# Half of a weight matrix on 32 partitions by four DMA engines, its product as one row, and fifteen tiny loads from ScalarE's queue

## The chip, the cores and the metric

The kernel runs on one core of one Trainium2 chip. The metric is the device time of an execution in microseconds (us), of which medians over several executions are quoted. The span that a profile gives is about 2 us shorter than the time, because it runs from the first to the last instruction. All runs of this study were in the fast state, so fast runs are compared with fast runs throughout.

## The reference, cut to what matters

A single token `x` of 512 values goes through an attention over a window of 4096 cached positions for 32 heads, and through a small MLP whose result gates the attention.

```python
xn = _layernorm(x)
# attention: q = xn @ wq; softmax(q k^T) v over the last 4096 positions, 32 heads of 128; @ wo
s = _A_ref(xn, k_cache, v_cache, wq, wo)
# gate
h  = gelu(layernorm(xn) @ w1)
g0..g3 = h shifted by one or two positions, forward and back
hs = concatenate([g0, g1, g2, g3]) @ w2      # 512 x 512
x1 = xn + hs
h2 = gelu(layernorm(x1) @ w3) @ w4           # 512 x 1376, 1376 x 512
g  = silu(x1 + h2)
return x + s * g
```

With one position every shift moves all of `h` out, so what is multiplied by `w2` is zero. The kernel still loads `w2` and does the product, with a vector of zeros. That matters for the experiments: the order in which the rows of `w2` lie cannot change the result.

The bytes are nearly all in the caches and weights: 67.1 MB of K and V in 64 loads of 1024 KB, `wq` and `wo` with 4.2 MB each, and 3.3 MB of `w2`, `w3` and `w4` (`w1` is not loaded).

## The kernel before

The program first issues the loads of `x`, from ScalarE, and of the weights, from SyncE, whose helper `load` keeps them in program order.

```python
    x_bf = small.tile([P, KC], BF16, name="x_bf")
    nc.scalar.dma_start(out=x_bf[:], in_=A_x.rearrange("a b (p c) -> p (a b c)", p=P))
    x_row = small.tile([P, P], BF16, name="x_row")
    nc.gpsimd.memset(x_row[:], 0.0)
    nc.scalar.dma_start(out=x_row[0:P:32, :], in_=A_x.rearrange("a b (j n) -> (a b j) n", j=KC))
    w2_sb = wts.tile([P, KC, D], BF16, name="w2_sb")
    load(w2_sb[:], B_w2.rearrange("(p c) n -> p c n", p=P))
    w3_sb = wts.tile([P, KC, F], BF16, name="w3_sb")
    load(w3_sb[:], B_w3.rearrange("(p c) n -> p c n", p=P))
    # ... three loads of w4, one of wq
```

The product with `w2` fills four columns, and its result is added to the normalized `x`. The sum `x1_f` starts the second half of the MLP.

```python
    for j in range(KC):
        for c in range(KC):
            nc.tensor.matmul(hs_ps[:, j:j + 1], lhsT=w2_sb[:, c, j::4],
                             rhs=shifted_bf[:, c:c + 1], start=(c == 0), stop=(c == KC - 1))
    x1_f = small.tile([P, KC], FP32, name="x1_f")
    nc.vector.tensor_tensor(out=x1_f[:], in0=xn_f[:], in1=hs_ps[:], op=ALU.add)
```

Some sums are opened by a matmul that writes zeros. It reads an identity matrix, which GpSimd makes.

```python
    def rows_open(ps):
        nc.tensor.matmul(ps[:], lhsT=zero_bf[:], rhs=ident_bf[:], start=True, stop=False,
                         skip_group_check=True)
```

The loop then loads a K tile per head and, four heads later, a V tile. The V tiles reuse the memory of the MLP's and q's weights, so the first V load has to wait for the last matmul that reads `wq`.

```python
    for i in range(H + LAG):
        if i < H:
            k_head(i, load_kv(k_pool, A_k_cache, i))
        if i == LAG:
            wts_guard.__exit__(None, None, None)
            v_pool = ctx.enter_context(tc.tile_pool(name="v", bufs=V_BUFS))
        if i >= LAG:
            v = load_kv(v_pool, A_v_cache, i - LAG)
            # ... wo loads, v_head
```

Of the kernel before, what the change touches and what calls it, by code (L numbers as in the profile page):

```python
# [9 lines left out]
P = 128  # L10
BF16 = mybir.dt.bfloat16
FP32 = mybir.dt.float32
ACT = mybir.ActivationFunctionType
ALU = mybir.AluOpType
# [5 lines left out]
G = 4  # L20
LAG = 4
K_BUFS = 12
V_BUFS = 7


@with_exitstack
def kernel(
# [14 lines left out]
    nc = tc.nc  # L42

    Bb, Sq, D = A_x.shape
# [9 lines left out]
    KC = D // P  # L54
# [5 lines left out]
    small = ctx.enter_context(tc.tile_pool(name="small", bufs=1))  # L60
    ps_misc = ctx.enter_context(tc.tile_pool(name="ps_misc", bufs=1, space=PSUM))
    ps_tr = ctx.enter_context(tc.tile_pool(name="ps_tr", bufs=3, space=PSUM))
    ps_s = ctx.enter_context(tc.tile_pool(name="ps_s", bufs=2, space=PSUM))
    ps_o = ctx.enter_context(tc.tile_pool(name="ps_o", bufs=1, space=PSUM))
    ps_y = ctx.enter_context(tc.tile_pool(name="ps_y", bufs=1, space=PSUM))
    k_pool = ctx.enter_context(tc.tile_pool(name="k", bufs=K_BUFS))
    kt_pool = ctx.enter_context(tc.tile_pool(name="kt", bufs=2))
# [3 lines left out]
    wts = wts_guard.__enter__()  # L71

    def load(dst, src):
        return tc.keep_in_program_order(nc.sync.dma_start(out=dst, in_=src))
# [3 lines left out]
    x_row = small.tile([P, P], BF16, name="x_row")  # L78
    nc.gpsimd.memset(x_row[:], 0.0)
    nc.scalar.dma_start(out=x_row[0:P:32, :], in_=A_x.rearrange("a b (j n) -> (a b j) n", j=KC))  # L80
    w2_sb = wts.tile([P, KC, D], BF16, name="w2_sb")
    load(w2_sb[:], B_w2.rearrange("(p c) n -> p c n", p=P))
    w3_sb = wts.tile([P, KC, F], BF16, name="w3_sb")
    load(w3_sb[:], B_w3.rearrange("(p c) n -> p c n", p=P))
    w4_sb = wts.tile([P, 11, D], BF16, name="w4_sb")
    load(w4_sb[:, 0:8, :], B_w4[0:8 * P, :].rearrange("(p c) n -> p c n", p=P))
    load(w4_sb[:, 8:10, :], B_w4[8 * P:10 * P, :].rearrange("(p c) n -> p c n", p=P))
# [4 lines left out]
    def load_kv(pool, cache, h):  # L92
        t = pool.tile([P, NC, Dh], BF16, tag="kv", name="kv")
        load(t[:], cache[0, h, W0:, :].rearrange("(p c) d -> p c d", p=P))
        return t
# [5 lines left out]
    ones_f = const.tile([P, P], FP32, name="ones_f")  # L101
# [26 lines left out]
# [4 lines that stand above are left out]
    def rows_add(ps, col, w, last):  # L132
        k = col.shape[0]
        for j in range(KC):
            nc.tensor.matmul(ps[32 * j:32 * j + 1, :], lhsT=col, rhs=w[0:k, j * P:(j + 1) * P],  # L135
                             start=False, stop=last, skip_group_check=True)
# [28 lines left out]
    xn_f = small.tile([P, KC], FP32, name="xn_f")  # L165
# [5 lines left out]



    shifted_bf = small.tile([P, KC], BF16, name="shifted_bf")
    nc.vector.memset(shifted_bf[:], 0.0)
    hs_ps = ps_misc.tile([P, KC], FP32, tag="misc", name="hs_ps")
    for j in range(KC):
        for c in range(KC):
            nc.tensor.matmul(hs_ps[:, j:j + 1], lhsT=w2_sb[:, c, j::4],
                             rhs=shifted_bf[:, c:c + 1], start=(c == 0), stop=(c == KC - 1))  # L180
    x1_f = small.tile([P, KC], FP32, name="x1_f")
    nc.vector.tensor_tensor(out=x1_f[:], in0=xn_f[:], in1=hs_ps[:], op=ALU.add)  # L182
    xc3, _, rstd3 = ln_stats(x1_f[:], "z3")
    z3_bf = small.tile([P, KC], BF16, name="z3_bf")
    nc.vector.tensor_scalar(out=z3_bf[:], in0=xc3[:], scalar1=rstd3[:], scalar2=None, op0=ALU.mult)

    hsr_ps = ps_misc.tile([P, P], FP32, tag="misc", name="hsr_ps")
    rows_open(hsr_ps)
    for c in range(KC):
        rows_add(hsr_ps, shifted_bf[:, c:c + 1], w2_sb[:, c, :], c == KC - 1)  # L190
    x1_row = small.tile([P, P], FP32, name="x1_row")
    nc.vector.tensor_scalar(out=x1_row[:], in0=x_row[:], scalar1=negmean[:], scalar2=rstd[:],
                            op0=ALU.add, op1=ALU.mult)
# [6 lines left out]
    for j, (m, cols) in enumerate(chunks):  # L200
        for c in range(KC):
            nc.tensor.matmul(a_ps[0:m, j:j + 1], lhsT=w3_sb[:, c, cols], rhs=z3_bf[:, c:c + 1],  # L202
                             start=(c == 0), stop=(c == KC - 1))
# [15 lines left out]
    for h in range(1, H, 2):  # L219
        for c in range(KC):  # L220
            nc.tensor.matmul(qT_ps[:, h:h + 1], lhsT=wq_sb[:, c, h * Dh:(h + 1) * Dh],  # L221
                             rhs=xn_bf[:, c:c + 1], start=(c == 0), stop=(c == KC - 1))
# [4 lines left out]
    for i in range(0, H // 2, 4):  # L227
        qb_ps = ps_tr.tile([P, 4, Dh], FP32, tag="pt", name="qb_ps")
        for c in range(KC):
            nc.tensor.matmul(qb_ps[:], lhsT=xn_rep[:, c, :], rhs=wq_h[:, c, 2 * i:2 * i + 8:2, :],  # L230
                             start=(c == 0), stop=(c == KC - 1))
# [16 lines left out]
    def flush():  # L248
        while pending:
            qk(*pending.pop(0))  # L250

    def k_head(h, kn):
        g, hl = divmod(h, G)
        if hl == 0:
            st[g] = {
                "sT": ps_s.tile([P, G // 2, NC], FP32, tag="sT", name="sT"),
                "sS": sm_pool.tile([P, G // 2, NC], FP32, tag="sS", name="sS"),
            }
        s = st[g]
        if h % 2 == 0:  # L260
            prod = prod_pool.tile([P, NC, Dh], BF16, tag="prod", name="prod")
            nc.vector.tensor_tensor(out=prod[:], in0=kn[:],  # L262
                                    in1=q_bc[:, h // 2:h // 2 + 1, :].to_broadcast([P, NC, Dh]),
                                    op=ALU.mult)
            nc.vector.tensor_reduce(out=s["sS"][:, hl // 2, :], in_=prod[:], axis=AX.X, op=ALU.add)  # L265
        else:
            kt = kt_pool.tile([P, NC, P], BF16, tag="kt", name="kt")
            for b in range(NB):
                pt = ps_tr.tile([P, 8, P], BF16, tag="pt", name="pt")
                for i in range(8):  # L270
                    nc.tensor.transpose(pt[:, i, :], kn[:, b * 8 + i, :], ident_bf[:])  # L271
                nc.scalar.copy(out=kt[:, b * 8:(b + 1) * 8, :], in_=pt[:])  # L272
                if b == 0:
                    flush()
            pending.append((s["sT"], hl, h, kt))
            if hl == G - 1:
                flush()
        if hl == G - 1:
            softmax(g)
# [33 lines left out]
    def load_wo(i):  # L313
        h0, n = blocks[i]
        rows = A_wo[h0 * P:(h0 + n) * P, :]
        if n == 8:
            t = k_pool.tile([P, n, D], BF16, tag="kv", name="wo_8")
        else:
            t = v_pool.tile([P, n, D], BF16, tag=f"wo{i}", bufs=1, name="wo_4")
        wo_blk[i] = t  # L320
        if i < last_block:
            load(t[:], rows.rearrange("(p t) n -> p t n", p=P))
        else:
            rows = rows.rearrange("(h p) n -> p h n", p=P)
            load(t[:, 0:n - 1, :], rows[:, 0:n - 1, :])
            load(t[:, n - 1, :], rows[:, n - 1, :])
# [59 lines left out]
    for i in range(H + LAG):  # L386
        if i < H:
            k_head(i, load_kv(k_pool, A_k_cache, i))
        if i == LAG:
            wts_guard.__exit__(None, None, None)  # L390
            v_pool = ctx.enter_context(tc.tile_pool(name="v", bufs=V_BUFS))
        if i >= LAG:
            h = i - LAG
            v = load_kv(v_pool, A_v_cache, h)
            if h + 1 in (b[0] for b in blocks):
                load_wo(block_of[h])
            if h == H - 1:
                load_wo(last_block)
            v_head(h, v)
# [38 lines left out]
```

## Time and profile before

| quantity | before |
|---|---|
| time, beside the changed kernel | 198.97 us, median of 4 (198.35 to 199.78) |
| span of the profiled execution | 196.8 us |
| bytes of weights and caches | 78.85 MB |
| their rate between 50 and 180 us | 421 GB/s |
| the sum x1 | 14.00 us |
| the first V load is issued | 30.13 us |
| the last `wo` load lands, first to last of the 16 engines | 188.50 to 193.18 us |

The profile's lines for this kernel stand in the prediction below. To read them: the GB/s line has 40 slices of 4.92 us, and any slice well below 420 is time that the DMA engines did not use. In the lists of waits the three numbers are the total in us, the count, and the longest. The kernel is one stream of bytes at a steady rate. Its end moves when the stream loses time; apart from that, the last of the 16 engines ends 1.6 to 2.7 us behind their mean in the kernels below.

One more number is needed below, and the prediction lacks it. All that is queued ahead of the first V load is `w2`, `w3`, `w4`, `wq` and five K tiles, 12.78 MB. In this trace 12.74 MB have moved at 33.5 us. The first V load, issued at 30.13, has its first bytes at about 31.2 if it takes 1.03 us as the first weight load did (0.72 to 1.75). So the engines had 2.3 us of work left when the V data arrived. That is the whole reserve of the first V load.

### The profile page before, as it was taken

To read this page: it belongs to the slowest core of one execution; us is meant where nothing else is said; L and a number is where in the kernel's file an instruction comes from. 1 tells how busy PE (TensorE), PEld (TensorE's weight loads), DVE (VectorE), ACT (ScalarE), POOL (GpSimd) and SP (SyncE) were. 2 spreads that over 40 slices of the span, in tenths; PEclk is the share of its full clock that TensorE was granted. 3 is DMA by queue.
4 is the path that set the end of the run, shared out by engine and by line. 5 is a ranking of instruction groups with operands and counts; after the bars stand their busy time and mean duration, and the time that the engine had idled before them with its cause. 6 is when DMAs were issued, how large, how long until landed. Compare 5 with 4: busy or idle time off the path is not lost.

```text
span 196.8 us, 5237 instructions
## 1 busy us (share of the span) xinstructions
PE 119.4 (61%) x2399; PEld 108.4 (55%) x2399; DVE 126.9 (64%) x140; ACT 69.3 (35%) x82; POOL 4.9 (3%) x17
## 2 busy tenths in 40 slices
PE   0315896851969474684829293756665654929443
PEld 0314745841969473583829292656565653929332
DVE  1225049998959993959387937959198929594301
ACT  2000329742565243070707070242525250707000
POOL 1011000000000000000000000000000000000000
PEclk9999999695585555576766667555555585575555
DMA  6999899999999999999999999999999999999960
GB/s 185 383 485 446 355 416 421 426 426 421 426 421 423 421 421 425 423 425 420 426 421 428 421 425 416 425 420 426 423 428 423 425 418 425 421 426 422 426 268 10
DMA packets 11349, 79.17 MB, mean 402 GB/s; under 512 B 1376, under 2 KB 1984, under 8 KB 2368
## 3 DMA queue, kind: packets, MB, share of 16 engines
q1 hardware_dynamic: 11176, 78.85, 96.3%
q8 instruction: 18, 0.29, 0.6%
q10 hardware_dynamic: 152, 0.00, 0.0%
q14 instruction: 3, 0.02, 0.0%
HBM read 78.84 MB, written 0.00 MB: 401 GB/s over the span
## 4 chain that ended last, share of the span: by engine, by line
DMA 71%; DVE 12%; issue 6%; PE 6%; ACT 2%; POOL 1%; SPq 0%; POOLq 0%
DMA kv<-in_A_v_cache_dram 40%; DMA kv<-in_A_k_cache_dram 30%; DVE sS L265 7%; DVE prod L262 3%; ACT kt L272 1%; PE a_ps L202 1%; PE qT_ps L221 1%; PE oT L364 1%; PE qb_ps L230 1%; PE h_ps L135 1%; PE y_ps L135 0%; PE ln_ps L140 0%; PE ln_ps L152 0%; ACT q_bc L232 0%; POOL ln_rstd_x L158 0%
## 5 line engine op out<-in xcount | busy, mean ns | idle before, releaser
L272 ACT COPY kt<-pt 128x1024 bf16<-128x1024 bf16 x64 | 60.2, 1025 | 73.0 <-PE pt L271 73.0
L265 DVE TENSOR_REDUCE sS<-prod 128x32 f32<-128x4096 bf16 x16 | 70.7, 4419 | 0.5
L271 PE MATMUL pt<-ident_bf,kv 128*128 128x128 bf16 x512 | 53.8, 298 | 18.2 <-DMA kv<-in_A_k_cache_dram 17.7
L271 PEld LDWEIGHTS <-kv 128*128 128x128 bf16 x512 | 49.8, 140 | 19.7 <-DMA kv<-in_A_k_cache_dram 18.7
L364 PEld LDWEIGHTS <-kv 128*128 128x128 bf16 x1024 | 30.0, 102 | 30.5 <-DMA kv<-in_A_v_cache_dram 22.8
L262 DVE TENSOR_TENSOR prod<-kv,q_bc 128x4096 bf16<-128x4096 bf16 x16 | 36.5, 2283 | 11.0 <-DMA kv<-in_A_k_cache_dram 8.8
L364 PE MATMUL oT<-pT,kv 128*128 128x1 bf16 x1024 | 32.6, 165 | 17.6 <-DMA kv<-in_A_v_cache_dram 17.3
L243 PE MATMUL sT<-qT_bf,kt 128*128 128x1 bf16 x512 | 20.4, 166 | 2.6 <-ACT kt L272 2.3
L243 PEld LDWEIGHTS <-kt 128*128 128x128 bf16 x512 | 18.3, 103 | 3.4 <-ACT kt L272 3.2
L300 PE MATMUL den_ps<-pT,ones_bf 128*128 128x128 bf16 x8 | 2.0, 253 | 16.9 <-ACT pT L294 16.9
L371 DVE TENSOR_TENSOR o<-oT,rden 128x4 bf16<-128x4 f32 x7 | 1.1, 162 | 17.3 <-PE oT L364 17.3
L294 ACT ACTIVATE pT<-e 128x128 bf16<-128x128 f32 x8 | 2.5, 309 | 16.5 <-DVE e L290 16.5
L140 PEld LDWEIGHTS ln_ps<-x_f,ones_f 128*128 128x128 f32 x4 | 1.0, 312 | 11.3 <-DVE x_f L182 6.4
L287 POOL PARTITION_ALL_REDUCE mb<-m x8 | 3.0, 373 | 162.5 <-DVE m L285 162.5
L205 ACT ACTIVATE a_bf<-a_ps 128x10 bf16<-128x10 f32 x1 | 0.2, 180 | 17.4 <-PE a_ps L202 17.4
L302 DVE TENSOR_REDUCE den<-den_ps 128x4 f32<-128x128 f32 x8 | 2.3, 292 | 5.5 <-PE den_ps L300 5.5
L135 PEld LDWEIGHTS <-ox 128*1 128x1 bf16 x112 | 2.5, 113 | 5.3 <-DVE ox L341 5.3
L367 DVE TENSOR_TENSOR o<-oT,rden 128x1 bf16<-128x1 f32 x4 | 0.6, 161 | 7.2 <-PE oT L364 7.2
L230 PE MATMUL qb_ps<-wq_sb,xn_rep 128*128 128x512 bf16 x16 | 5.2, 497 | 0.0
L135 PE MATMUL y_ps<-wo,ox 128*1 128x128 bf16 x112 | 3.7, 306 | 2.3 <-DVE ox L341 2.3
L140 PE MATMUL ln_ps<-x_f,ones_f 128*128 128x4 f32 x4 | 1.2, 365 | 5.9 <-DVE x_f L163 4.9
L290 DVE TENSOR_TENSOR e<-sS,mb 128x64 f32<-128x64 f32 x8 | 1.8, 224 | 3.9 <-POOL mb L287 3.9
(79 smaller groups left out, 48.2 us busy)
## 6 DMA issues: line engine op xcount, KB each, us to landing
kv<-in_A_k_cache_dram SPq DMA_DIRECT2D x32, 1024.0 KB, 19.7
kv<-in_A_v_cache_dram SPq DMA_DIRECT2D x32, 1024.0 KB, 19.7
wq_sb<-in_A_wq_dram SPq DMA_DIRECT2D x1, 4096.0 KB, 19.2
wo<-in_A_wo_dram SPq DMA_DIRECT2D x3, 1024.0 KB, 20.4
w_sb<-in_B_w_dram SPq DMA_DIRECT2D x1, 1376.0 KB, 7.9
w_sb<-in_B_w_dram SPq DMA_DIRECT2D x1, 1024.0 KB, 10.2
w_sb<-in_B_w_dram SPq DMA_DIRECT2D x1, 512.0 KB, 3.7
wo<-in_A_wo_dram SPq DMA_DIRECT2D x1, 512.0 KB, 19.8
```

The costliest lines, as they stand in the source:

```text
L135: nc.tensor.matmul(ps[32 * j:32 * j + 1, :], lhsT=col, rhs=w[0:k, j * P:(j + 1) * P], start=False, stop=last, skip_group_check=True)
L140: nc.tensor.matmul(ps[:], lhsT=ones_f[:], rhs=src_f, start=True, stop=True)
L230: nc.tensor.matmul(qb_ps[:], lhsT=xn_rep[:, c, :], rhs=wq_h[:, c, 2 * i:2 * i + 8:2, :], start=(c == 0), stop=(c == KC - 1))
L243: nc.tensor.matmul(sT[:, hl // 2, c:c + 1], lhsT=kt[:, c, :], rhs=qT_bf[:, h:h + 1], start=True, stop=True)
L262: nc.vector.tensor_tensor(out=prod[:], in0=kn[:], in1=q_bc[:, h // 2:h // 2 + 1, :].to_broadcast([P, NC, Dh]), op=ALU.mult)
L265: nc.vector.tensor_reduce(out=s["sS"][:, hl // 2, :], in_=prod[:], axis=AX.X, op=ALU.add)
L271: nc.tensor.transpose(pt[:, i, :], kn[:, b * 8 + i, :], ident_bf[:])
L272: nc.scalar.copy(out=kt[:, b * 8:(b + 1) * 8, :], in_=pt[:])
L287: nc.gpsimd.partition_all_reduce(mb[:], m1[:], channels=P, reduce_op=ReduceOp.max)
L294: nc.scalar.activation(out=pT[:], in_=e[:], func=ACT.Exp, scale=scale)
L302: nc.vector.tensor_reduce(out=den[:], in_=den_ps[:], axis=AX.X, op=ALU.add)
L364: nc.tensor.matmul(oT[:, k:k + 1], lhsT=v[:, c, :], rhs=s["pT"][:, hl % 2, hl // 2, c:c + 1], start=(c == 0), stop=(c == NC - 1))
```

## The change

Its intent, as it reads: the four lowest DMA engines end earlier than the others, so give them a larger share by laying half of `w2` on 32 partitions in two loads with an outer dimension of 4. Since these rows are now in 16-partition pieces, the product is made as one row of 512 and then turned into columns. Fifteen loads of pieces of `x` on 15 down to 1 partitions, whose data nobody reads, are issued from ScalarE's queue in the loop. `w3` now goes ahead of `w2`.

```diff
-    w2_sb = wts.tile([P, KC, D], BF16, name="w2_sb")
-    load(w2_sb[:], B_w2.rearrange("(p c) n -> p c n", p=P))
     w3_sb = wts.tile([P, KC, F], BF16, name="w3_sb")
     load(w3_sb[:], B_w3.rearrange("(p c) n -> p c n", p=P))
+    R2 = 8 * 8 * NE                                      # NE = 4
+    w2_lo = wts.tile([32 + 4 * NE, 8, D], BF16, name="w2_lo")
+    for c in range(2):
+        load(w2_lo[32 * c:32 * c + 4 * NE], B_w2[c * R2 // 2:(c + 1) * R2 // 2, :].rearrange(
+            "(b a r) n -> a b (r n)", b=4, a=NE))
+    C2 = (D - R2) // P
+    w2_hi = wts.tile([P, C2, D], BF16, name="w2_hi")
+    load(w2_hi[:], B_w2[R2:D, :].rearrange("(p c) n -> p c n", p=P))
 ... (w4, wq as before)
-    shifted_bf = small.tile([P, KC], BF16, name="shifted_bf")
+    shifted_bf = small.tile([P, 1], BF16, name="shifted_bf")
-    (16 matmuls of one column into hs_ps)
+    lo = [[w2_lo[32 * c:32 * c + 4 * NE, r, :] for r in range(8)] for c in range(2)]
+    hs = small.tile([1, D], FP32, name="hs")
+    for p0, ws in ((0, lo[0] + [w2_hi[:, r, :] for r in range(C2)]), (32, lo[1])):
+        hs_ps = ps_tr.tile([1, D], FP32, tag="pt", name="hs_ps")
+        for i, w in enumerate(ws):
+            nc.tensor.matmul(hs_ps[:], lhsT=shifted_bf[p0:p0 + w.shape[0], :], rhs=w, ...)
+        (copy into hs, then add)
+    hc_ps = ps_misc.tile([P, KC], FP32, tag="misc", name="hc_ps")
+    for c in range(KC):
+        nc.tensor.matmul(hc_ps[:, c:c + 1], lhsT=hs[:, c::KC], rhs=ones_f[0:1, 0:1], start=True, stop=True)
 ...
         if i < H:
             k_head(i, load_kv(k_pool, A_k_cache, i))
+        if 6 <= i < 21:
+            mk = small.tile([21 - i, 32], BF16, name=f"mk{i}")
+            nc.scalar.dma_start(out=mk[:], in_=A_x.rearrange("a b (p n) -> (a b p) n", p=16)[0:21 - i, :])
```

More of the change, by code (lines that the diff above doesn't have):

```diff
@@ L22 @@
 K_BUFS = 12
+NE = 4
 V_BUFS = 7
@@ L170 @@
     nc.vector.tensor_copy(out=xn_rep[:], in_=xn_bf[:].unsqueeze(2).to_broadcast([P, KC, P]))
-    shifted_bf = small.tile([P, KC], BF16, name="shifted_bf")
+    shifted_bf = small.tile([P, 1], BF16, name="shifted_bf")
     nc.vector.memset(shifted_bf[:], 0.0)
-    hs_ps = ps_misc.tile([P, KC], FP32, tag="misc", name="hs_ps")
-    for j in range(KC):
-        for c in range(KC):
-            nc.tensor.matmul(hs_ps[:, j:j + 1], lhsT=w2_sb[:, c, j::4],
-                             rhs=shifted_bf[:, c:c + 1], start=(c == 0), stop=(c == KC - 1))
+    lo = [[w2_lo[32 * c:32 * c + 4 * NE, r, :] for r in range(8)] for c in range(2)]
[3 more added lines that the diff above has]
+        for i, w in enumerate(ws):
+            nc.tensor.matmul(hs_ps[:], lhsT=shifted_bf[p0:p0 + w.shape[0], :], rhs=w, start=(i == 0),
+                             stop=(i == len(ws) - 1))
+        if p0 == 0:
+            nc.vector.tensor_copy(out=hs[:], in_=hs_ps[:])
+        else:
+            nc.vector.tensor_tensor(out=hs[:], in0=hs[:], in1=hs_ps[:], op=ALU.add)
+    hc_ps = ps_misc.tile([P, KC], FP32, tag="misc", name="hc_ps")
+    for c in range(KC):
+        nc.tensor.matmul(hc_ps[:, c:c + 1], lhsT=hs[:, c::KC], rhs=ones_f[0:1, 0:1], start=True, stop=True)
     x1_f = small.tile([P, KC], FP32, name="x1_f")
-    nc.vector.tensor_tensor(out=x1_f[:], in0=xn_f[:], in1=hs_ps[:], op=ALU.add)
+    nc.vector.tensor_tensor(out=x1_f[:], in0=xn_f[:], in1=hc_ps[:], op=ALU.add)
     xc3, _, rstd3 = ln_stats(x1_f[:], "z3")
@@ L188 @@
     rows_open(hsr_ps)
-    for c in range(KC):
-        rows_add(hsr_ps, shifted_bf[:, c:c + 1], w2_sb[:, c, :], c == KC - 1)
+    rows_add(hsr_ps, ones_f[0:1, 0:1], hs, True)
     x1_row = small.tile([P, P], FP32, name="x1_row")
```

## The prediction

> **What bounds the kernel now.** I read the page's slices and DMA queues first, then the chain that ended last, the waits of the DMA queue, and the timeline of the first 36 us and of the last 13.
>
> ```profile
> DMA  6999899999999999999999999999999999999960
> GB/s 185 383 485 446 355 416 421 426 426 421 426 421 423 421 421 425 423 425 420 426 421 428 421 425 416 425 420 426 423 428 423 425 418 425 421 426 422 426 268 10
> ...
> q1 hardware_dynamic: 11176, 78.85, 96.3%
> q8 instruction: 18, 0.29, 0.6%
> ...
> DMA 71%; DVE 12%; issue 6%; PE 6%; ACT 2%; POOL 1%; SPq 0%; POOLq 0%
> ```
>
> The DMA row is at 9 in nearly every slice and GB/s lies at 416 to 428 from slice 6 to slice 38; 71% of the chain that ended last is DMA. 78.85 MB at about 423 GB/s take 186.4 us of the 196.8 us span. No compute engine is over 64%. So this is one long stream, and the end of the program is: when the stream starts to flow, plus the bytes over the rate, plus whatever one engine of the 16 lags behind, plus a fixed tail.
>
> ```profile
> SPq L74 <- DMA kv<-in_A_v_cache_dram: 59.4, 28, 3.3
> SPq L74 <- DMA kv<-in_A_k_cache_dram: 59.2, 28, 2.9
> ...
> SPq L74 <- PE qb_ps L230: 7.7, 1, 7.7
> ...
> SPq L74 <- DMA x_row<-in_A_x_dram: 1.6, 1, 1.6
> ...
> SPq L74 <- DMA x_bf<-in_A_x_dram: 1.1, 1, 1.1
> ```
>
> In these waits the SyncE queue waits 28 times each for a K and a V load: every load waits for the one eight before it, because the program has eight DMA semaphores which all its DMAs take in turn, those issued by ScalarE too. That is why the queue waits for x_row and x_bf at all, and it will decide this case.
>
> ```profile
> 0.72 2.36 SPq L74 DMA_DIRECT2D w_sb<-in_B_w_dram  x5
> 0.72 0.41 ACTq L77 DMA_DIRECT2D x_bf<-in_A_x_dram  x1
> ...
> 1.18 1.07 ACTq L80 DMA_DIRECT2D x_row<-in_A_x_dram  x1
> ...
> 4.67 0.17 DVE L163 CAST x_f<-x_bf 128x4 f32<-128x4 bf16 x1 [3.45 <-DMA x_bf<-in_A_x_dram]
> ...
> 12.63 0.28 POOL masks.py:199 TENSOR_SCALAR_AFFINE_SELECT ident_bf<-ident_bf 128x128 bf16<-128x128 bf16 x1 [11.57 <-issue]
> ...
> 14.00 0.15 DVE L182 TENSOR_TENSOR x_f<-xn_f,hs_ps 128x4 f32<-128x4 f32 x1
> ...
> 24.90 5.19 PE L230 MATMUL qb_ps<-wq_sb,xn_rep 128*128 128x512 bf16 x16
> ...
> 30.13 0.33 SPq L74 DMA_DIRECT2D kv<-in_A_v_cache_dram  x1
> ```
>
> The columns are start, duration, engine, line, operation, tiles, and in brackets the idle time before it and its releaser. Five weight loads go out in 2.36 us with no wait, so the stream never starves. x_bf needs 0.41 us to issue and lands after 3.9 us; x_row, on 4 partitions, needs 1.07 us. GpSimd is stuck until 12.63, so x's normalization cannot end before 13.5, and the first MLP addition (x_f at 14.00) has w2 long before. The first V load waits for the last q matmul, 30.13, which frees the weights' memory.
>
> ```profile
> 191.93 1.01 PE L364 MATMUL oT<-pT,kv 128*128 128x1 bf16 x32 [1.45 <-DMA kv<-in_A_v_cache_dram]
> ...
> 193.90 0.29 DVE L406 TENSOR_TENSOR out_row<-y,x_row 128x128 bf16<-128x128 f32 x1
> 194.22 0.65 SPq L74 DMA_DIRECT2D out_dram<-out_row  x1
> ```
>
> The last V load is what the last oT matmuls wait for, and 2.3 us after them the result is sent. From single semaphore increments in the trace: the 16 engines finish the last load of wo between 188.50 and 193.18 us. After the first one the others lag by 0.14, 0.34, 0.78, 0.84, 1.10, 1.68, 2.32, 3.02, 3.09, 3.12, 3.17, 3.18, 3.32, 4.65 and 4.68 us. Following these lags from load to load, each of the 16 KB instruction fetches (queue q8) sets one engine back by about 1.5 us, in turn over only 8 of the engines; each of the 8 is hit twice and two of them a third time. Four others were set back about 1 us early, when x_row's four packets came: those must be the lowest four. So two overtaxed engines that are not the lowest four set the end; an even share would finish at about 190.7 us.
>
> **What the Trainium skill says.** Its page "DMA: Bandwidth & Descriptors", section "Why a DMA increments its semaphore by 16 and not by 1", says that a DMA is spread over the largest number up to 16 that divides the slowest dimension of both sides, on the lowest-numbered engines. With an outer dimension of 4 in the source each w2_lo load thus runs on 4 engines; x_row's four packets agree. The section "Queues, rings and completion order" says that an engine alternates between its queues by packets, and the trace agrees: x_bf's 8-byte packets stand one by one between the 4 KB packets of w2. The section "Issuing engines are not separate DMA queues" says that loads from ScalarE share the same engines and only save issue time. So neither the tiny loads nor the order can add bandwidth here.
>
> **The change part by part.** Bytes hardly change: w2 is still 512 KB, the tiny loads are 7.7 KB.
>
> *Balance.* w2_lo is 256 KB on 4 engines, 64 KB each where they had 16 KB; the other 12 carry 16 KB less. At 423/16 = 26.4 GB/s that is 0.6 us less on each of the 12, among them the two that end last, and 1.8 us more on the lowest four, which ended at least 2.3 us ahead of those two. Alone this would gain 0.6 us. It looks like the intent.
>
> *The tiny loads.* In the source they stand at the loop's heads 6 to 20. In the built order they don't: nothing they read is late, so the scheduler puts all 15 right behind x_row, before ScalarE's first activation. The semaphores are then dealt out so: x_bf 0, w3 1, x_row 2, the first five tiny loads 3 to 7, the sixth 0 (after x_bf), the seventh 1 (after w3 has landed), w2_lo's first half 2 (after x_row), tiny loads 8 to 12 on 3 to 7, the 13th 0, w2_lo's second half 1 (after the 7th tiny load), the 14th 2, the 15th 3, w2_hi 4 (after the 9th), the three w4 loads 5, 6, 7 (after the 10th, 11th, 12th), wq 0 (after the 13th). So the big stream stands behind a string of tiny loads, each of which ScalarE has to issue, one at a time, from the moment that w3 has landed.
>
> Its times. w3 is issued at 0.72 and flows from 1.75 (as w2 did). The first packet of a queue took about 1.1 us and the 11 KB packets 0.413 us, 8 per engine: 1.75 + 1.1 + 7 x 0.413 = 5.75, and 0.35 us to its landing: 6.1. x_bf's eight packets per engine now alternate with those of w3, so it lands with it. ScalarE issues x_bf and x_row until 2.25. For a tiny load I choose 0.75 us (x_row 1.07, the output's 0.65 on SyncE, x_bf 0.41): the first five until 6.05, then the sixth from 6.1, the 7th from 6.85, the 9th from 8.35, the 10th from 9.1, the 13th from 11.35. From the start of an issue to landing, without other traffic, the output's store took about 1.65 us (194.22 to 195.87). So w2_lo's second half may go at 8.5, w2_hi at 10.0, w4 at 10.75, wq at 13.0. First bytes come 1.03 us after issue (0.72 to 1.75): w2_hi at 11.05, w4 at 11.8, wq at 14.0, when w4 isn't through yet. Counted from 11.2 us (11.05, and a gap of 0.15 before w4) the stream flows without a break.
>
> By then only w3 (1.41 MB) and w2_lo (0.26 MB, only on four engines, in time that would be idle) have come. The other 77.2 MB take 182.5 us at 423 GB/s: 193.7 for the first engine to finish, against 188.2 of data now. That is 5.5 us later. Some of the loss at the start (first-packet latency, x_row's setback) is paid in the hole and not again, up to 1 us of it. The 0.6 us of balance is in the 77.2 MB already. I take +5.3.
>
> *hs.* The 16 small matmuls and the 16 of hsr go, 18 matmuls of 512 columns, two passes of one row on VectorE and 8 small fp32 matmuls come. A 512-column matmul took 5.19/16 = 0.32 us, mostly at half clock. After w2_hi (about 12.1 landed) six are left, 2 us, then the passes and transposes, 2 us as I estimate: x1 at about 16 instead of 14. The chain to the last q matmul moves by 2 to 3 us, and wq lands later itself (14.8 + 9.9 us = about 25), so V's first load leaves at about 33. The K loads before it keep the engines busy until 37 or so. So it stays off the path.
>
> *The tail* is the same: the same two engines, the same last matmuls.
>
> **The rivals.** (a) The tiny loads cost nothing because they are tiny, and the balance wins 0.6 us or more: 198.5. For it: x_bf's packets took 9 ns each. Against: the cost is in the waits, which are in the built program. (b) The issue of a tiny load is as slow as x_row's 1.07 us, or one takes 3 to 5 us to land as x_bf and x_row did under load: the hole ends at 13.8 or later, +8 us, 207.5 and above. (c) ScalarE issues them in 0.41 us each: w2_hi at 9.4, +3.8 to +4.7, 203.3 to 204.2, at the border. (d) Each semaphore write of a foreign queue stalls its engine (after x_row's the next packet took 0.83 to 1.45 us instead of 0.41): in the middle of the stream engine 0 would lose 15 us. But they run in the hole; I give it little. (e) Late hs delays the first V load into a second hole: at least 3 us later than I reckon would be needed.
>
> **Range and chances.** The sum is 199.5 + 5.3 = 204.8 us. Rival (c) sets the low end, less half a microsecond for luck in the tail: 202.3. Rival (b) sets the high end: 209. The border of 2% is 203.5, 1.3 us below my value; with most of the uncertainty upward I give 0.79 to slower, 0.2 to the same, 0.01 to faster.
>
> **What would show it.** In the changed profile GB/s should fall from 383 to some 150 in slice 1 and from 485 to some 330 in slice 2, and later slices stay near 423; the DMA queue should wait for tiny loads (mk) between 6 and 13 us; ScalarE should issue 15 of them by 13 us; w4's first issue at 10 to 12 us; V's first at about 33 without a gap in GB/s; the last V landing at 197. I am wrong if the tiny loads are issued and landed by 8 us, if there is a hole later than 15 us, or if the engines' last increments spread by more than 6 us.

## The result, and the profile after

The changed kernel took 205.49 us (median of 4, 204.33 to 206.56) against 198.97 us. The ratio is 1.0324, with a 95% interval of 1.0246 to 1.0401: it is slower. A ratio here is the mean time of one kernel's fast runs over the mean of the other's fast runs of the same rounds, so it is not quite the ratio of the medians quoted. The output is correct. The profiled execution has a span of 202.5 us, so its slices are 5.06 us.

From the page of the changed kernel, the slices, two DMA queues, and the shares of the chain that ended last:

```profile
DMA  6269999999999999999999999999999999999970
GB/s 207 99 237 430 479 369 419 403 404 424 424 434 417 426 426 426 426 424 424 424 424 426 424 426 422 424 427 422 422 426 422 426 426 424 419 429 416 422 278 14
...
q1 hardware_dynamic: 11216, 78.85, 93.8%
...
q10 hardware_dynamic: 392, 0.01, 0.1%
...
DMA 59%; DVE 19%; PE 13%; issue 6%; ACT 2%; POOL 1%; SPq 0%; POOLq 0%
```

What the first three slices (207, 99 and 237) lack would take 8.7 us at 424 GB/s, and from slice 9 on the flow stays near 424. The same 78.85 MB now fill the 16 engines for 93.8% of the span where they filled 96.3%: 12.6 us are idle (6.2% of 202.5) instead of 7.3 us (3.7% of 196.8). The difference, 5.3 us, accounts for most of the 5.7 us by which the span grew. Queue q10 carries the loads from ScalarE in 0.1% of the time, so the tiny loads cost the engines nothing by their bytes.

From the waits of SyncE's DMA queue:

```profile
SPq L75 <- PE qb_ps L247: 9.0, 1, 9.0
...
SPq L75 <- DMA x_row<-in_A_x_dram: 5.9, 1, 5.9
SPq L75 <- DMA mk<-in_A_x_dram: 2.7, 2, 1.9
```

The waits for x_row (before the first half of `w2`) and for two tiny loads (mk) are new or longer. They stand ahead of all weight loads but one. The wait for the last q matmul, which is the first V load's, has grown from 7.7 to 9.0 us.

From the timeline of the first 40 us (start, duration, engine, line, operation, tiles, count, and in brackets the idle time before it and its releaser):

```profile
2.30 9.00 ACTq L408 DMA_DIRECT2D mk<-in_A_x_dram  x15
...
7.00 2.19 SPq L75 DMA_DIRECT2D w_lo<-in_B_w_dram  x2
...
11.02 3.78 PE L190 MATMUL hs_ps<-w_lo,shifted_bf 16*1 16x512 bf16 x12
11.14 0.35 SPq L75 DMA_DIRECT2D w_hi<-in_B_w_dram  x1
...
11.54 1.37 SPq L75 DMA_DIRECT2D w_sb<-in_B_w_dram  x3
...
12.96 0.63 SPq L75 DMA_DIRECT2D wq_sb<-in_A_wq_dram  x1
...
20.35 0.16 DVE L200 TENSOR_TENSOR x_f<-xn_f,hc_ps 128x4 f32<-128x4 f32 x1 [2.11 <-PE hc_ps L198]
...
36.16 0.33 SPq L75 DMA_DIRECT2D kv<-in_A_v_cache_dram  x1
```

ScalarE needs from 2.30 to 11.30 us for the fifteen tiny loads, though they were written into the loop. `w3` had landed by 6.7, and `w2_hi`, the next load that uses all engines, leaves at 11.14. Then x1 comes at 20.35 instead of 14.00, and the first V load at 36.16 instead of 30.13.

From the timeline of the end:

```profile
197.79 1.02 PE L381 MATMUL oT<-pT,kv 128*128 128x1 bf16 x32 [1.57 <-DMA kv<-in_A_v_cache_dram]
...
199.74 0.29 DVE L426 TENSOR_TENSOR out_row<-y,x_row 128x128 bf16<-128x128 f32 x1
200.06 0.59 SPq L75 DMA_DIRECT2D out_dram<-out_row  x1
```

From the last attention matmul to the result's store it is 2.27 us, as it was (191.93 to 194.22 is 2.29). The tail is only shifted.

**Where the time went.** The trace has every packet of the weight and cache queue. From these I count the bytes moved up to a moment, and call lost time the difference between that moment and the time that these bytes take at 422.5 GB/s. Before, 3.2 us are lost up to 20 us and 0.1 us between 30 and 45 us. After, 8.8 us and 0.6 us. The growth is 5.6 us in the start and 0.5 us later, 6.1 in all. The mean landing of the last `wo` load over the 16 engines moved by the same amount, from 190.71 to 196.79. The steady rate is the same (421.3 and 422.6 GB/s between 50 and 180 us, and the 8 KB packets take 309 ns in both). So everything is lost before 45 us.

### The profile page after: what moved, and what is told of

It reads as the page before. It is cut to its first block, busy times and chain, and to the rows that moved or that the text cites. A ratio compares the mean times of both kernels' runs of the same rounds, so it can differ in the third digit from the quotient of the medians.

```text
span 202.5 us, 5261 instructions
## 1 busy us (share of the span) xinstructions
PE 126.3 (62%) x2401; PEld 109.7 (54%) x2401; DVE 128.7 (64%) x142; ACT 69.3 (34%) x82; POOL 4.9 (2%) x17
## 3 DMA queue, kind: packets, MB, share of 16 engines
q1 hardware_dynamic: 11216, 78.85, 93.8%
HBM read 78.85 MB, written 0.00 MB: 389 GB/s over the span
## 4 chain that ended last, share of the span: by engine, by line
DMA 59%; DVE 19%; PE 13%; issue 6%; ACT 2%; POOL 1%; SPq 0%; POOLq 0%
DMA kv<-in_A_v_cache_dram 29%; DMA kv<-in_A_k_cache_dram 29%; DVE sS L282 11%; DVE prod L279 6%; PE hs_ps L190 3%; PE pt L288 2%; ACT kt L289 1%; PE oT L381 1%; PE a_ps L219 1%; PE hc_ps L198 1%; PE qT_ps L238 1%; PE qb_ps L247 1%; PE h_ps L144 1%; PE sT L260 1%; DVE hs L195 0%
## 5 line engine op out<-in xcount | busy, mean ns | idle before, releaser
L288 PE MATMUL pt<-ident_bf,kv 128*128 128x128 bf16 x512 | 52.7, 295 | 17.3 <-DMA kv<-in_A_k_cache_dram 16.7
L288 PEld LDWEIGHTS <-kv 128*128 128x128 bf16 x512 | 49.0, 140 | 18.7 <-DMA kv<-in_A_k_cache_dram 17.7
L381 PEld LDWEIGHTS <-kv 128*128 128x128 bf16 x1024 | 29.8, 102 | 31.7 <-DMA kv<-in_A_v_cache_dram 23.5
L190 PE MATMUL hs_ps<-w_lo,shifted_bf 16*1 16x512 bf16 x16 | 5.6, 618 | 0.0
```

The lines of the kernel that those rows point to most:

```text
L190: nc.tensor.matmul(hs_ps[:], lhsT=shifted_bf[p0:p0 + w.shape[0], :], rhs=w, start=(i == 0), stop=(i == len(ws) - 1))
L288: nc.tensor.transpose(pt[:, i, :], kn[:, b * 8 + i, :], ident_bf[:])
L381: nc.tensor.matmul(oT[:, k:k + 1], lhsT=v[:, c, :], rhs=s["pT"][:, hl % 2, hl // 2, c:c + 1], start=(c == 0), stop=(c == NC - 1))
```

## The experiments

Twelve kernels ran, each beside the kernel before on the same chip, whose median was 198.4 to 198.7 us. All gave the right result. Two explanations stood against each other at first. The first is the prediction's: the tiny loads sit in the line of DMA semaphores ahead of the big loads, and all else is harmless. The second is the prediction's rival (e): the product with `w2` comes late, so the first V load comes late, and there is a hole in front of it.

### Removing the tiny loads

```diff
 # the changed kernel
-        if 6 <= i < 21:
-            mk = small.tile([21 - i, 32], BF16, name=f"mk{i}")
-            nc.scalar.dma_start(out=mk[:], in_=...)
```

> The changed kernel without its 15 tiny loads; the 4-engine load of w2 and hs as a row stay. Theory (the whole loss is the start's hole, made by big loads that take a semaphore after a tiny load): the weights are issued one behind the other again, the hole from 6 to 12 us is gone, and what is left is the balance, 0.6 us: 198.4 us or a ratio to before of 0.997 (0.992 to 1.002). Rival (the 4-engine load, or the later hs, makes part of the loss): 201 us or more.

Measured: 203.66 us, ratio 1.0271 (1.0225 to 1.0317). The expectation fell: only 1 of some 6 us came back. Its slices, its wait for the q matmul and its timeline:

```profile
GB/s 203 370 447 417 413 419 268 140 424 422 424 427 422 427 422 427 426 421 421 426 426 424 422 422 424 421 427 422 424 422 427 422 426 417 424 426 422 429 290 12
```

```profile
SPq L75 <- PE qb_ps L247: 13.4, 1, 13.4
```

```profile
12.00 0.27 PE L138 MATMUL y_ps<-ident_bf,zero_bf 128*128 128x128 bf16 x1 [2.29 <-POOL ident_bf masks.py:199]
...
12.20 3.57 PE L190 MATMUL hs_ps<-w_lo,shifted_bf 16*1 16x512 bf16 x12
...
21.32 0.16 DVE L200 TENSOR_TENSOR x_f<-xn_f,hc_ps 128x4 f32<-128x4 f32 x1 [2.12 <-PE hc_ps L198]
...
37.07 0.33 SPq L75 DMA_DIRECT2D kv<-in_A_v_cache_dram  x1
```

The start is repaired: slices 1 and 2 are at 370 and 447. But slices 6 and 7, 30 to 40 us, have fallen to 268 and 140. The DMA queue waits 13.4 us for the last q matmul and sends the first V load at 37.07, when the data queued ahead of it (12.74 MB) has been through since 35.0; the flow is below 150 GB/s from 34.0 to 38.5 us. Lost time is 3.4 us up to 20 us and 5.3 us between 30 and 45. So there are two holes that the change can make, and the first one hides the second. In the changed kernel the late start delays the queued bytes until 39.0 us, so that a first V load whose bytes come at about 37.2 (36.16 and 1.03) is in time.

The timeline shows why the chain is late: the first product with `w2` is at 12.20, right behind the matmul that zeroes `y_ps`, which stands ahead of it in the tensor engine's order and waits for GpSimd's identity matrix.

### The tiny loads alone

```diff
 # the kernel before
+        if 6 <= i < 21:
+            mk = small.tile([21 - i, 32], BF16, name=f"mk{i}")
+            nc.scalar.dma_start(out=mk[:], in_=...)
```

> The kernel before with the 15 tiny loads alone. In the built program w2 and w3 go out without a wait, w4 waits for the third tiny load, its second and third part for the 9th and the 10th (which waits for w3), wq for w4 itself. Theory (waits): w2 and w3 flow until 7.5 us, w4 starts at about 8.2, wq at about 12: holes of 1 and 1 us, ratio 1.010 (1.005 to 1.016), 201 us. Rival (the tiny loads' packets and semaphore writes cost engine time wherever they run): the same 6.5 us as in the changed kernel, 205.5 us. Rival (only the order and the 4 engines matter): 199.

Measured: 203.38 us, ratio 1.0235 (1.0199 to 1.0272). The direction was as expected, the size was not. The slices and the waits:

```profile
GB/s 207 201 329 345 418 420 428 415 423 429 421 431 423 415 436 415 434 416 425 426 418 433 420 428 425 423 428 416 429 423 423 425 423 428 421 423 418 419 234 8
```

```profile
SPq L74 <- DMA mk<-in_A_x_dram: 10.0, 3, 7.2
```

Here the hole is at the start alone: slices 1 to 3 at 201, 329 and 345, with 10.0 us of waits for tiny loads, and 420 from slice 4 on. Lost time is 7.6 us up to 20 us, 4.4 more than before, and nothing later. The first V load leaves only at 35.48, because here the q matmuls wait for `wq` itself, until 27.47, but the queued bytes last until 37.7. So the prediction's mechanism is real and is worth 4.4 us by itself.

### Five tiny loads instead of fifteen

```diff
 # the changed kernel
-        if 6 <= i < 21:
+        if 6 <= i < 11:
```

> The changed kernel with the first 5 tiny loads only: none of them waits, and the big loads take their semaphores after x_bf, w3, x_row and the five, all of which land by about 7.3 us. Theory (waits): w2_hi is issued at about 8.6 instead of 11.1, the stream flows 2.5 us earlier than in the changed kernel: 203 us, ratio 1.019 (1.013 to 1.025). Rival (each tiny load costs its share): a third of 6.5 us, 201.2, ratio 1.011.

Measured: 204.86 us, ratio 1.0311 (1.0271 to 1.0351), a miss. The big loads do leave earlier (`w2_hi` at 8.72), and the start loses 7.7 us instead of 8.8. But this kernel streamed more slowly afterwards, 418.0 GB/s between 50 and 180 us, with 8 KB packets of 312 ns instead of 309. Over the 63.2 MB after 45 us that is 1.6 us, which agrees with the mean landing of the last load (6.3 us later than before, of which 4.7 are lost by 45 us). Why it streams more slowly stays open.

### All of w2 by eight engines, without tiny loads

```diff
 # the changed kernel, without the tiny loads
-NE = 4
+NE = 8
-    (w2_hi and its load; its matmuls)
```

> No tiny loads, and all of w2 on the lowest 8 engines (64 KB each where they had 32). In the trace of before 8 engines take all the instruction fetches and the lowest four are not among them; the numbers of the 8 are not shown. If they are 8 to 15, each has 32 KB or 1.2 us less to bring, and the end comes 1.2 us before that of the kernel before: 197.8 us, ratio 0.994, and 0.6 us better than without tiny loads at 4 engines. If some of the 8 lie below 8, those end 1.2 us later: 200.2 us.

Measured: 201.97 us, ratio 1.0169 (1.0122 to 1.0215), a miss for the same reason: first V load at 36.91, 5.2 us lost between 30 and 45. It is 1.7 us better than the version on four engines, and part of this may be the balance that the change was after. In the profiled executions the last engine ends 1.6 us behind the mean of the 16 here, 2.2 us with four engines, and 2.5 us before. The table below shows how far to trust this: another kernel with all of `w2` on eight engines (e13) has 2.6.

### Only the row

```diff
 # the kernel before; w2 loaded whole and first, as there
-    (16 matmuls of one column into hs_ps, 16 of hsr)
+    for c in range(KC):
+        nc.tensor.matmul(hs_ps[:], lhsT=shifted_bf[:], rhs=w2_sb[:, c, :], ...)
+    (copy into hs; four transposing matmuls; rows_add of hs)
```

> The kernel before with hs as one row alone: w2 stays whole on 128 partitions, so 4 matmuls of 512 columns instead of 18. They can run from 7.2 us: 4 x 0.43, a pass of 0.68, 8 transposing matmuls in 2.0 make 11.6 us, before x is normalized at 13.5. Theory: off the path, ratio 1.000 (0.995 to 1.005). Rival (a row is slow by its pass and its transposes): x1 2.7 us later, ratio 1.007 or more.

Measured: 198.3 us, ratio 0.9973 (0.9954 to 0.9993), as expected. The four matmuls of 512 columns run at 6.80, ahead of the wait for GpSimd, x1 comes at 12.36, and the first V load leaves at 28.75. So the form as a row is harmless by itself. In the change it is late because it needs 18 such matmuls, and because `w2` comes later.

### Moving the chain alone, without tiny loads

This edit lets the zeroing matmul multiply zeros by zeros, so that it needn't wait for GpSimd. The result is the same.

```diff
 # the changed kernel, without the tiny loads
     def rows_open(ps):
-        nc.tensor.matmul(ps[:], lhsT=zero_bf[:], rhs=ident_bf[:], ...)
+        nc.tensor.matmul(ps[:], lhsT=zero_bf[:], rhs=zero_bf[:], ...)
```

> The changed kernel without tiny loads (ratio 1.027), with one edit: the matmul that zeroes y is fed by zeros, so hs need not wait for GpSimd's identity. hs can start when w2_lo has landed, at about 9 us instead of 12.2, so x1 and the first V load move 2.5 to 3 us forward (37.1 to about 34.3). Theory (the hole before the V load is as long as the chain is late): ratio 1.014 (1.009 to 1.019). Rival (the chain does not set the time): stays at 1.027.

Measured: 201.38 us, ratio 1.0149 (1.0126 to 1.0173), as expected. Its slices:

```profile
GB/s 199 390 451 423 400 419 280 313 424 423 429 426 421 423 429 421 421 424 426 423 424 424 421 428 418 426 428 416 431 419 431 418 423 418 428 421 424 426 293 13
```

No load was moved. x1 comes at 19.21 instead of 21.32, the first V load at 34.56 instead of 37.07, and slice 7 rises from 140 to 313. Lost time between 30 and 45 us falls from 5.3 to 3.0 us, and the time by 2.3 us. This is the test that shows the late chain as a cause of the second hole.

### Moving the chain further, with w2 ahead of w3

```diff
 # the version just shown
-    w3_sb = ...; load(w3_sb ...)
     (w2_lo, w2_hi and their loads)
+    w3_sb = ...; load(w3_sb ...)
```

> The changed kernel without tiny loads, w2 loaded before w3, and the matmul that zeroes y fed by zeros instead of the identity, so that the tensor engine no longer stands until GpSimd's identity at 12 us in front of the hs matmuls. Theory (in the run without tiny loads it was the late hs chain that cost 5 us, by the V load waiting for the weights' memory): hs starts at about 5 and ends at 13, x1 at about 16 instead of 21.3, the first V load leaves at 32 instead of 37 and the hole at 30 to 40 us shrinks to 1 us or less: ratio 1.001 (0.995 to 1.008). Rival (the 4-engine load costs it): stays at 1.027.

Measured: 200.87 us, ratio 1.0108 (1.0059 to 1.0157). Its slices:

```profile
GB/s 38 379 447 429 412 417 422 419 422 419 432 421 426 422 419 424 421 430 421 426 422 426 421 429 419 424 426 419 424 427 426 424 419 426 419 426 426 425 258 9
```

The second hole is gone, as expected: x1 at 16.24, the first V load at 32.63, 0.1 us lost between 30 and 45. But the ratio lies above the expected range. A new cost of 1.9 us has come up at the start, most of it in slice 0, which has 38 GB/s where the kernel before has 185. `w2_lo` leaves first, and the wide loads behind it start late: `w2_hi` is issued at 2.24 and has its first packet at 4.43, `w3` at 2.73 and 5.90. So issue to first packet is 2.2 and 3.2 us where the first load of the kernel before has 1.03. How the queue works there is not visible in the trace.

### The balance alone, in the kernel before

Two kernels bring half of `w2` by four engines, or all of it by eight, into the same tile as before.

```diff
 # e7: the kernel before
-    load(w2_sb[:], B_w2.rearrange("(p c) n -> p c n", p=P))
+    load(w2_sb[0:64], B_w2[0:D // 2, :].rearrange("(b a c) n -> a b (c n)", b=16, a=4))
+    load(w2_sb[64:P], B_w2[D // 2:D, :].rearrange("(p c) n -> p c n", p=64))
 # e8: the kernel before
-    load(w2_sb[:], B_w2.rearrange("(p c) n -> p c n", p=P))
+    load(w2_sb[:], B_w2.rearrange("(b a c) n -> a b (c n)", b=16, a=8))
```

> The kernel before, with half of w2 brought by the lowest 4 engines into the same tile: no tiny loads, no row, w2 first. New theory: the change made two holes of about 5 us that lie one over the other, one in front of the weights (tiny loads), one in front of the first V load (the hs chain ends 6 to 7 us late); the 4-engine load itself costs nothing. Then only the balance is left: ratio 0.997 (0.993 to 1.001), 197.9 us. Rival (four engines alone at the start delay the weights): 1.01 or more.

> The kernel before, with all of w2 brought by the lowest 8 engines into the same tile. If the 8 engines with the instruction fetches are 8 to 15, they carry 32 KB less, 1.2 us: ratio 0.994 (0.989 to 0.998), 197.3 us, faster than both kernels. If not, those of them below 8 end 1.2 us later: 1.006.

Measured: 201.81 us, ratio 1.0138 (1.0091 to 1.0185) with four engines, and 200.88 us, ratio 1.0103 (1.0059 to 1.0147) with eight. Both are misses. They lose 3.5 and 2.7 us more than before up to 20 us, and their slices 0 are at 60 and 94 GB/s. In both, as in the experiment before this, a narrow load stands at the head of the queue. Its packets show a second effect. In the kernel with eight engines the 4 KB packets of `w2` take 159 ns in the median, as before the change, while they are alone (2.8 to 3.6 us). From 3.64, when `w3` flows beside them, they take 341 ns, and the 11 KB packets of `w3` take 1015 ns until `w2` is through at 7.3, and 413 from 7.8 on. The first V load is at 33.87 and 32.62, and no second hole follows.

### The balance behind w3

To take the narrow load away from the head, `w3` goes first, and the zeroing matmul needs no identity.

```diff
 # the kernel before
     def rows_open(ps): rhs=zero_bf[:] instead of ident_bf[:]
-    w2_sb = ...; load(w2_sb ...)
     w3_sb = ...; load(w3_sb ...)
+    w2_sb = ...; (e13: the load on eight engines as in e8)
+                 (e16: the two loads as in e7)
```

> The kernel before with w3 loaded first, then all of w2 on the lowest 8 engines into the same tile, and the matmul that zeroes y fed by zeros (so that hs does not stand behind GpSimd's identity). Theory: a load on few engines costs 2 to 3 us only where it stands first in the queue and nothing else flows; behind w3 it is hidden. The first V load leaves at about 30, no hole, and the balance gains up to 1.2 us: ratio 0.994 (0.989 to 0.999), 197.4 us. Rival (the narrow load holds up the weights behind it wherever it stands): 1.007 or more.

> The same with half of w2 on the lowest 4 engines, as the change has it. Theory: ratio 0.997 (0.992 to 1.001), so the 4-engine load behind w3 costs nothing and gains about 0.6 us, and all of the loss is in the two holes. Rival: 1.007 or more.

Measured: 203.18 us, ratio 1.0228 (1.0200 to 1.0257) with eight, and 201.57 us, ratio 1.0154 (1.0128 to 1.0180) with four engines. Both are misses. The slices of the one with eight:

```profile
GB/s 204 231 318 434 407 412 419 347 411 427 422 429 424 417 432 417 424 429 416 425 427 421 427 425 417 422 430 414 434 421 421 427 425 414 429 423 416 434 273 9
```

Slices 1 and 2 are at 231 and 318 with no tiny load in the program, so there is a third way to a hole. The 4 KB packets of `w2` take 341 ns in the median, where they take 159 in the kernel before, and the 8 KB packets of the `w4` load behind it take 640 ns where they take 309. With four engines it is 295 and 545 ns. In the changed kernel and in the versions made from it, the 8 KB packets up to 18 us have medians of 309 to 314 ns. One difference between them is where an engine writes. By the edits, each low engine writes 16 neighbouring partitions in these two kernels and in the two before them. The change writes blocks of four at a distance of 32, and that is the pattern which the Trainium skill gives, for a load of 128 partitions, as the one in which each engine writes one port of the memory (page "DMA: Bandwidth & Descriptors", section "The descriptor swizzle"). Another difference is the order in which the rows of `w2` are read; but in the experiment before this the same order cost nothing, 159 ns, as long as nothing else flowed. So the doubled packets fit engines that meet at the ports, but no run here isolates that: it is argued. What is shown is the doubling, and that it comes with other traffic. `wq` is late in both kernels, the first V load leaves at 35.38 and 34.92, and the table below has a small second hole for them.

### The tiny loads in the running stream

A copy of one element of that step's K tile into `mk` holds each tiny load in the loop, where it was written.

```diff
 # the changed kernel
         if 6 <= i < 21:
             mk = small.tile([21 - i, 32], BF16, name=f"mk{i}")
+            nc.scalar.copy(out=mk[0:1, 0:1], in_=kn[0:1, 0, 0:1])     # kn: the tile that load_kv returned
             nc.scalar.dma_start(out=mk[:], in_=...)
```

> The changed kernel with the tiny loads kept at their places in the loop: before each, ScalarE writes one element of the K tile of this step into its tile, so it cannot go before that K has landed. No tiny load is at the start, so the loss without tiny loads (ratio 1.027, by the late V load) remains. If a semaphore write of ScalarE's queue sets its engine back 0.9 us in the running stream, as x_row's did, engine 0 loses up to 13.5 us in 15 of them and ends some 9 to 10 us after the engines that end last: 213 us. If tiny loads cost nothing in the stream: 203.7 us.

Measured: 205.59 us, ratio 1.0363 (1.0329 to 1.0397). Neither expectation holds, though the small one is nearer. Its slices and waits:

```profile
GB/s 208 382 397 422 414 421 274 155 348 427 422 427 347 407 431 419 429 422 427 422 424 424 426 422 430 418 430 419 427 421 427 421 429 424 421 429 413 422 321 29
```

```profile
SPq L75 <- DMA mk<-in_A_x_dram: 41.8, 12, 9.3
```

The hole at the start is gone and the second is there, as without tiny loads. Against the version without them it is 1.9 us slower. SyncE waits twelve times for a tiny load, 41.8 us in all and up to 9.3 us, and slices 8 and 12 are dented to 348 and 347. So fifteen loads of a few bytes cost about 2 us in the stream, and far from the 15 us that rival (d) would make of them. The dents and the slower rate between 50 and 180 us (418.9 GB/s) could be both the waits and the engines' interruptions; which it is stays open.

### All kernels side by side

The columns are: time lost up to 20 us and between 30 and 45 us, both beyond the kernel before; how much later the last `wo` load lands in the mean of the engines; by how much the last engine lies behind that mean; and the measured loss, which is the ratio less 1 times 198.5 us. The first four are from the one profiled execution, good to about 0.1 us, the last from all runs.

| kernel | start | 30 to 45 us | mean landing | last behind mean | measured loss |
|---|---|---|---|---|---|
| before | 0 | 0 | 0 | 2.5 | 0 |
| the change | 5.6 | 0.5 | 6.1 | 2.2 | 6.4 |
| e1: no tiny loads | 0.2 | 5.2 | 5.2 | 2.2 | 5.4 |
| e15: and zeros for the identity | -0.1 | 2.9 | 2.8 | 1.9 | 3.0 |
| e12: and w2 first | 1.9 | 0.0 | 1.8 | 2.5 | 2.1 |
| e6: no tiny loads, eight engines | 0.1 | 5.1 | 5.0 | 1.6 | 3.4 |
| e3: five tiny loads | 4.5 | 0.4 | 6.3 | 2.1 | 6.2 |
| e5: tiny loads in the stream | 0.5 | 5.9 | 7.5 | 1.6 | 7.2 |
| e2: tiny loads alone | 4.4 | -0.1 | 4.4 | 2.7 | 4.7 |
| e9: row alone | -0.5 | 0.0 | -0.5 | 2.5 | -0.5 |
| e7: four engines, w2 first | 3.5 | -0.1 | 4.2 | 2.4 | 2.7 |
| e8: eight engines, w2 first | 2.7 | -0.1 | 2.7 | 2.0 | 2.0 |
| e13: eight engines after w3 | 3.3 | 1.0 | 4.2 | 2.6 | 4.5 |
| e16: four engines after w3 | 3.1 | 0.5 | 3.5 | 1.6 | 3.1 |

The sum of the two holes gives the mean landing, except for the two kernels with a slower stream (e3, e5) and for e7, which lost another 0.6 us between 20 and 30 us. The mean landing, with what the spread gained, gives the measured loss within 1 us, except for e7, whose profiled execution took 203.29 us, 1.5 above its median. No version beats the kernel before by 2%: the row alone is 0.3% faster. The change, e1, e3 and e5 are slower by more than 2% over their whole interval.

## Why the prediction was right or wrong

**The total was right.** 204.8 us was predicted, within 202.3 to 209.0, and 205.49 was measured. "So the big stream stands behind a string of tiny loads" is what the waits show, and the tiny loads alone (e2) lose 4.4 us at the start with no other part of the change present. The rival "The tiny loads cost nothing because they are tiny" is refuted by the same run. The prediction's hole was 5.5 us for the first engine to finish, taken as 5.3. Measured were 6.0 (188.50 to 194.52). Part of the nearness is luck: the sum starts from 199.5 us, the median known then, and the kernel before took 198.97 beside the changed one, so the growth was 6.5 us where 5.3 was predicted. The low end of the range has a slip, without effect here: rival (c) less half a microsecond is 202.8, not 202.3.

**The times in the hole were right by errors that cancel.** "For a tiny load I choose 0.75 us" was too long: the fifteen issues took 0.24 to 0.55 us each, 0.32 in the median. "About 1.65 us" from the start of an issue to landing was too short for the loads that count. The ninth, which lets `w2_hi` go, was issued at 7.92, earlier than the 8.35 predicted, and `w2_hi` left at 11.14, 3.2 us later, instead of at 10.0. The semaphores show the wait itself: the two share one, as predicted, and the last of the ninth's increments comes at 11.12. Of its seven, three come at 9.62 to 9.69 and four only at 11.02 to 11.12. At that time the lowest engines were busy with `w2_lo`, so by these times the narrow load held `w2_hi` back by some 1.4 us. That the lowest four alone bring it, as the Trainium skill's rule quoted in the prediction has it, agrees with the semaphore records: the halves of `w2_lo` land in four increments each, between 10.66 and 10.74 and between 12.24 and 12.90 us, where `w3` has sixteen. `w2_hi`'s first packet then came at 12.11 where 11.05 was predicted.

**The step that failed is the one on *hs*.** The prediction said "x1 at about 16 instead of 14", "V's first load leaves at about 33" and "So it stays off the path". Measured were 20.35 and 36.16. The two mis-sized terms are these. The first twelve matmuls were taken to be over when `w2_hi` lands, but they began only at 11.02: the first half of `w2_lo` had landed at 10.74, and the zeroing of `y_ps` went in front at 10.82. All 18 took until 17.53, 6.5 us or 0.36 us each, so this part ended 3.4 us later than the 14.1 that the prediction's figures give. (Its remark "mostly at half clock" is a misreading: the granted clock was 1.00 from 24.9 to 30.1 us in the kernel before, and 1.00 during these matmuls.) The two passes (0.68 and 0.67 us, one of them beside the matmuls) and the transposing matmuls (four in the code, eight in the trace, 2.02 us) then took 2.8 us in place of 2. From x1 to the first V load it is about 16 us in six traces (16.1 before, 15.8 after, 15.8 in e1, 15.4 in e15, 16.4 in e9 and e12), so there the delay of x1 goes right through to the V load. It does not where the q matmuls wait for `wq` instead, as in e2, where it is 22.7 us. In the changed kernel `wq` landed at 27.12, 1.9 us before the chain let the q matmuls start at 29.03. So with x1 on time the V load would still have left at about 34.3, by an estimate from these figures.

The conclusion held for the changed kernel, with 0.5 us lost there, by luck. Rival (e), "Late hs delays the first V load into a second hole", needed a V load "at least 3 us later" than 33, and it was 3.2 us later. No hole came of it because a second estimate was off too: the engines had work until 39.0 us, not "until 37 or so". Where the start is not late, the room is the 2.3 us of the kernel before, and the delay was 6. Without the tiny loads the same chain costs 5.2 us (e1), and moving it by 2.5 us gives 2.3 us back (e15). The prediction never asked what would be left if the first hole were closed, and so its account of the parts would have misled anyone who wanted to mend the kernel: each of the two causes alone costs about 5 us, and both together 6.4.

**The balance was over-rated.** "Alone this would gain 0.6 us": the last engine lay 2.47 us behind the mean before and 2.25 after, which is 0.2 us. Without tiny loads it is 2.17, and with all of `w2` on eight engines 1.58, 0.9 us better. But the kernels with the narrow load range from 1.6 to 2.6, and those without it have 2.5 to 2.7; these are single executions, so a gain is likely but not shown. It is small in any case beside what the narrow loads can cost at the start (e7, e8, e12).

**The other signs.** w4 left at 11.54 (10 to 12 predicted), and ScalarE was through by 11.30 ("by 13 us"). Slices 1 and 2 fell to 99 and 237, deeper than 150 and 330. The last V tile landed at 197.74 where 197 was predicted, and its matmuls began at 197.79; the engines' spread was 4.5 us, below the 6 that would have spoken against it.

## What to carry to other kernels

A DMA that nobody reads is not free if DMAs share a few semaphores in turn: look in the built program at what each big load waits for, since a scheduler may move small loads to the front. When a stream has a hole, ask what the next hole would be if this one were closed: measure how much work is still queued when the next dependent load arrives (here 2.3 us), and compare it with every delay that the change adds to that load's chain. Then test by removing one part and by adding that part alone, because two causes that hide each other look like one in either test.

## What the Trainium skill lacked or had wrong

- Page "DMA: Bandwidth & Descriptors", section "Where 436 GB/s comes from", says that for transfers between HBM and the on-chip memory the HBM side, about 358 GB/s, binds. Here one core streamed at 421 to 423 GB/s for 130 us; the page's own measured table has 425 GB/s for a single core and keeps the 358 for two cores streaming at once, and that is what this case agrees with.
- The same page says which engines a load on few engines uses. It lacks what such a load does to the loads behind it in its queue: with a narrow load at the head, the next wide loads had their first packets 2.2 and 3.2 us after issue, against 1.03 us (e12).
- The same page's section on the swizzle gives the pattern of partitions, and not what it costs to leave it: here 4 KB packets took 341 ns instead of 159, and the 8 KB packets behind them 640 instead of 309 (e13). That ports are the reason is not shown.
- Page "Runtime: NRT & Kernel Launch", section "Instruction fetch mechanics", calls the cost of crossing a 16 KB boundary in the instructions mostly hidden, and lacks what a fetch costs the DMA engine that carries it. In the kernel before, the packet of each of the 18 fetches takes 0.97 to 1.11 us, and by the lags that the prediction lists each fetch sets one engine back by about 1.5 us, on only 8 of the 16 engines. In a kernel bound by DMA that is not hidden: the last engine ends 2.5 us behind the mean.
- I found no page that says that small loads written in a loop can be placed ahead of the whole stream by the scheduler, where here they take the semaphores of the weight loads: 4.4 us lost (e2).
